# The first expert block on the seven-product scheme, with three sum banks and one side bank

## The chip, the cores and the metric

One core of one Trainium2 chip runs the whole program. The metric is the device time of one execution in microseconds. The engines are TensorE (PE, with its weight loads shown apart as PEld), VectorE (DVE), ScalarE (ACT), GpSimd (POOL) and SyncE (SP, which here issues nearly all the DMA transfers).

## The reference

Three stages follow one another: a feature-map attention, a dense layer pair, and a soft mixture of eight experts. Only the last one is touched by the change.

```python
def _moe2_ref(x, w_gate, w1, w2):            # x: 2304 x 512, w1: 8 x 512 x 1024, w2: 8 x 1024 x 512
    logits = x @ w_gate
    P = np.exp(logits - logits.max())
    for _ in range(8):                        # the balancing
        P /= P.sum(1, keepdims=True) + 1e-09
        P /= P.sum(0, keepdims=True) + 1e-09
        P *= N / E
    out = np.zeros((N, D))
    for e in range(E):
        ye = np.maximum(x @ w1[e], 0.0) @ w2[e]
        out += P[:, e:e + 1] * ye
    return out
```

## The kernel before

Every large product is made of three TensorE products (`mm3`, lines 79 to 82), since each operand is kept as a high and a low part. The expert stage runs over 16 blocks `b` (expert `e`, half `j` of its hidden columns), and each block over 3 units `c` of 768 tokens (`UP` = 3 pairs of token tiles). A unit (b, c) has a first product and a second one.

The first product (`hidden`) is a 2x2 block product in seven products (Strassen-Winograd). Its operands `t1, b11, b22, t2, b21, t3, t4` were stored to DRAM as `xs` by `operands` while the dense stage ended, and are read back through a ring of five buffers `xr`. Each of the seven is done for two column groups `q`, with 6 matmuls of 384 columns each, which makes 14 steps of one unit. Their sums live in banks `att` (2), `h` and `kv`.

The second product of a unit is interleaved with the 14 steps of the next unit. For blocks 1 to 15 it is again a seven-product scheme (`seconds`): seven operand pairs of `got` (made by `inner` and split into halves by ACT and POOL) and `w2t` (made by `w2_prep`), each for the three token pairs `i`, 6 matmuls of 256 columns each, so 126 matmuls a unit. DVE adds each result to `acc`. The sums lie in half banks of four PSUM banks `acc`. For block 0 (`b < FIRST`) it is the plain product (`outputs`): 6 token tiles a unit, 12 matmuls of 512 columns each, so 72 matmuls; ACT copies each result to `acc`. `w2_prep` then makes 4 weight tiles for block 0 and 7, with four extra sums (`combine`), for the other blocks.

In block 0 the gate logits are summed beside the first product (`gate_add`, 16 matmuls of 384 columns a unit) in a bank `acc` of its own and brought into token order by `gate_end`. The balancing, `sinkhorn`, is a generator with 11 stops. In the kernel before, both are advanced only inside `outputs` (lines 1039 to 1042), once for each call. The six calls that run in unit (1, 0) advance it four times, and nothing advances it later.

The scheduler of the framework orders the instructions of each engine's queue: by the place in the program text, lowered or raised by `high_priority`, and by when it expects operands and buffers to be free. Buffers with one tag share a number of slots: 8 for `w2o` (`W2B`), 14 for `h` (`HB`), 4 for `raw2`. The last two chunks of `operands` borrow slots of these: chunk 3 keeps its seven tiles `xo` in `w2o`, chunk 4 in `h`, until they are stored to `xs`.

Of the kernel before, what the change touches and what calls it, by code (L numbers as in the profile page):

```python
# [21 lines left out]
def tile_kernel(ctx: ExitStack, tc, q, k, v, w_phi, w_in, w_out, w_gate, w1, w2, out):  # L22
    nc = tc.nc
# [682 lines left out]
    FIRST = 1  # L706
# [57 lines left out]
    def w2_prep(b):  # L764
        def keep(o, src):
            w2t[b, o] = halves("w2o", W2B, src)

        if b < FIRST:
            for i in range(2 * QB):
                keep(i, raw.pop((b, True) + divmod(i, QB)))  # L770
                yield
            return
        (b11, b12), (b21, b22) = (tuple(raw.pop((b, True, r, k)) for k in range(2)) for r in range(2))
        keep("b11", b11)
        yield
# [12 lines left out]
        keep("b21", b21)  # L788
        yield
# [54 lines left out]
    out_pool = []  # L844
    lg = hp_.tile([P, NTT, E], F32, name="lg")
# [3 lines left out]
    def sinkhorn():  # L849
# [8 lines left out]
        ps = bank("acc")  # L858
# [3 lines left out]
        ps = bank("acc")  # L862
# [3 lines left out]
        for _ in range(NITER):  # L866
            nc.vector.tensor_reduce(out=r1, in_=pm, axis=AX.X, op=ALU.add)
            nc.vector.tensor_scalar(r1, r1, 1e-9, None, op0=ALU.add)
            nc.vector.reciprocal(out=r1, in_=r1)
            nc.vector.tensor_tensor(out=pm, in0=pm, in1=r1.unsqueeze(2).to_broadcast([P, NTT, E]), op=ALU.mult)  # L870
            nc.vector.tensor_reduce(out=c1, in_=pm.rearrange("p t e -> p e t"), axis=AX.X, op=ALU.add)
            yield
            ps = bank("acc")
# [24 lines left out]
    gate_ps = []  # L898
    GATE = {"t1": (0, 0), "b11": (0, 2 * E), "b22": (1, 0), "b21": (1, 4 * E)}

    def gate_add(x, kh, w0):
        first = not gate_ps
        if first:
            gate_ps.append(bank("acc"))
        for k in range(2):
            for h in range(2):
                nc.tensor.matmul(
                    gate_ps[0][0:4 * E, 0:UW], lhsT=wg[:, 2 * kh + k, w0:w0 + 4 * E], rhs=x[:, h, k, :],
                    start=first and k == 0 and h == 0, stop=True, skip_group_check=True,
                )  # L910

    def gate_end(c):
        lt = hp_.tile([4 * E, UW], F32, tag="u", name="lt", bufs=UB)
        nc.scalar.copy(lt, gate_ps.pop()[0:4 * E, 0:UW])
        yield
        ps = bank("acc")
        for i in range(UP):
# [4 lines left out]
            lg[:, 2 * UP * c:2 * UP * (c + 1), :], ps[:, 0:2 * UP * E].rearrange("p (t e) -> p t e", e=E)  # L922
# [3 lines left out]
    UB, HB = 10, 14  # L926

    side_work = []
# [54 lines left out]
    def hidden(b, c, n0, got):  # L983
# [11 lines left out]
        for i, o in enumerate(XOPS):  # L995
            x_ahead(n0 + i + XR)
            x = xring[n0 + i]
            for q in range(QB):
# [6 lines left out]
                if b == 0 and q == 0 and o in GATE:  # L1005
                    gate_add(x, *GATE[o])
# [6 lines left out]
                elif b >= FIRST:  # L1013
                    inner(b, o, q, T, got, ps, plus)
                elif o == "t2":
                    got["12", q] = relu_halves(plus("p53", q, ps))
                elif o == "b21":
                    T["c11", q] = plus("p1", q, ps)
                elif o == "t3":
                    got["22", q] = relu_halves(plus("p5", q, ps))  # L1020
                    if q == QB - 1:
                        for p in range(QB):
                            got["11", p] = relu_halves(T.pop(("c11", p)))
                else:
                    got["21", q] = relu_halves(ps)
                yield


    def outputs(b, ti, hs, t):
        _, acc, pm = out_pool  # L1030
        e, j = blocks[b]
        ps = bank("acc")
        ts_ = slice(t * P, (t + 1) * P)
        for i, h in enumerate(hs):
            w = w2t[b, i]
            mm3(ps, h[:, 0, ts_], h[:, 1, ts_], w[:, 0], w[:, 1], i == 0, i == 2 * QB - 1)
        a = acc[:, ti, :]
        nc.scalar.copy(a, ps)
        with tc.high_priority(offset=-100 if len(lg_done) == NUN else 50):
            if side_work and next(side_work[0], 1):  # L1040
                side_work.pop(0)
                lg_done.append(1)
# [5 lines left out]
    banks = []  # L1048

    def seconds(b, c, got):  # L1050
        _, acc, pm = out_pool
        e, j = blocks[b]
        if not banks:
            banks.extend(bank("acc") for _ in range(4))
# [3 lines left out]
        order = [SECOND[i] for i in ((0, 2, 1, 6, 4, 3, 5) if last else range(7))]  # L1058
        at_ = {
# [4 lines left out]
        if last:  # L1064
# [4 lines left out]
            }  # L1069
        seen, scaled = set(), set()  # L1070
        for ho, wo, ch, t, n in order:
            w = w2t[b, wo]
            due = []
            for i in range(UP):
                pb, half, first = at_[ch][i]
                first = bool(first) and ch not in seen
# [8 lines left out]
                for i_, ps in due:  # L1085
# [7 lines left out]
                    if e == 0:  # L1093
# [12 lines left out]
            seen.add(ch)  # L1106

    behind = []
    lg_done = []
    pending = None  # L1110
    n0 = 0
    for b, c in units:
        got = {}
        for i, _ in enumerate(hidden(b, c, n0, got)):
# [6 lines left out]
            elif odd and behind:  # L1121
                outputs(*behind.pop(0))
            if odd and c == NUN - 1 and b + 1 < len(blocks):
                take(coming, 1)
            if odd and c == 0 and b:
                take(late, 1)
        if not out_pool:
# [4 lines left out]
            take(w2_prep(0), 9)  # L1132
        n0 += len(XOPS)
        if b == 0:
            side_work.append(gate_end(c))
            next(side_work[-1])
            if c == NUN - 1:
                side_work.append(sinkhorn())
        if b >= FIRST:
            pending = seconds(b, c, got)  # L1140
        else:
            behind = [
                (b, 2 * (UP * c + i) + t, [got["%d%d" % (r, t + 1), q] for r in (1, 2) for q in range(QB)], i)
                for t in (1, 0) for i in range(UP)
            ]

        if c == 0:
            if b > 0:
                take(late, 9)
# [40 lines left out]
```

## Time and profile before

| | |
|---|---|
| median of 3 runs | 2093.19 us (2092.52 to 2093.55) |
| the profiled execution | 2092.61 us |
| its span, first to last instruction | 2090.8 us |
| PE busy | 2070.7 us, 99% |
| DVE, ACT, POOL busy | 67%, 44%, 57% |
| granted TensorE clock | 1.00 in every slice |

The span is the time between the first and the last instruction; the remaining 1.8 us of the execution lie around it. A share is an average over all stages. In the windows and timelines, times are counted from the span's start. The expert stage begins at 642 us.

### The profile page before, as it was taken

How to read it: one execution, taken by the hardware profiler on the slowest of the kernel's cores; microseconds unless marked ns; L12 is line 12 of the kernel's file. 1: busy time of each engine (PE TensorE's matmuls, PEld its weight loads, DVE VectorE, ACT ScalarE, POOL GpSimd, SP SyncE). 2: the span in 40 equal slices, each digit the busy share in tenths (PEclk: the TensorE clock that was granted, in tenths of full speed). 3: DMA queues.
4: the chain of work that ended last, by engine and by line, in shares of the span. 5: the costliest groups of instructions: out<-in, count | busy, mean ns of one | idle time of the engine just before them, and what ended most of it. 6: DMA issues, size and time to landing. Idle time of an engine off the chain costs nothing.

```text
span 2090.8 us, 36461 instructions
## 1 busy us (share of the span) xinstructions
PE 2070.7 (99%) x13433; PEld 1957.4 (94%) x13433; DVE 1395.0 (67%) x2547; ACT 922.6 (44%) x1892; POOL 1201.7 (57%) x1173
## 2 busy tenths in 40 slices
PE   8999999999999999999999999999999999999998
PEld 7787888888888899999999999999999999999998
DVE  8998765754324257766776677666776677667766
ACT  7776655654223334333433334333433343334432
POOL 2112211110301559987878788788787877879762
PEclk9999999999999999999999999999999999999999
DMA  8798565646736756565566655556556465654654
GB/s 264 256 331 284 173 189 167 203 140 217 262 121 194 249 177 226 212 213 211 181 222 226 213 202 205 208 211 232 197 212 222 172 233 220 216 214 175 241 189 135
DMA packets 194865, 440.02 MB, mean 210 GB/s; under 512 B 41448, under 2 KB 123496, under 8 KB 194688
## 3 DMA queue, kind: packets, MB, share of 16 engines
q1 hardware_dynamic: 190688, 428.19, 59.1%
q0 software_dynamic: 2560, 8.39, 1.0%
q8 instruction: 107, 1.75, 0.3%
q10 hardware_dynamic: 1440, 1.12, 0.2%
q14 instruction: 70, 0.57, 0.1%
HBM read 399.51 MB, written 38.12 MB: 209 GB/s over the span
## 4 chain that ended last, share of the span: by engine, by line
PE 92%; DVE 3%; ACT 2%; POOL 1%; issue 1%; DMA 1%; SPq 0%; POOLq 0%; DVEq 0%; ACTq 0%
PE ps_acc L82 14%; PE ps_acc L81 14%; PE ps_acc L80 13%; PE ps_att L80 6%; PE ps_att L81 6%; PE ps_att L82 6%; PE ps_h L80 6%; PE ps_h L82 6%; PE ps_h L81 6%; PE ps_kv L81 4%; PE ps_kv L80 4%; PE ps_kv L82 4%; PE ps_kv L86 1%; PE ps_att L86 1%; PE ps_acc L86 1%
## 5 line engine op out<-in xcount | busy, mean ns | idle before, releaser
L76 POOL TENSOR_TENSOR h<-u,h 128x384 fp32r<-128x384 f32 x450 | 509.1, 1149 | 169.8 <-ACT h L67 155.5
L81 PE MATMUL ps_acc<-w2o,h 128*128 128x256 f32 (+1 forms) x1950 | 557.0, 286 | 0.9 <-POOL w2o L76 0.8
L82 PE MATMUL ps_acc<-w2o,h 128*128 128x256 f32 (+1 forms) x1950 | 557.4, 286 | 0.4 <-POOL h L76 0.4
L80 PE MATMUL ps_acc<-w2o,h 128*128 128x256 f32 (+1 forms) x1950 | 555.2, 285 | 2.2 <-DVE acc L1097 1.7
L1097 DVE SCALAR_TENSOR_TENSOR acc<-ps_acc,pm,acc 128x256 f32<-128x256 f32 x876 | 378.7, 474 | 232.9 <-PE ps_acc L82 225.4
L67 ACT ACTIVATE h<-u 128x384 fp32r<-128x384 f32 x450 | 236.7, 526 | 328.6 <-DVE u L978 121.8
L81 PEld LDWEIGHTS ps_acc<-w2o,h 128*128 128x128 f32 x1950 | 368.4, 189 | 4.5 <-POOL w2o L76 2.2
L80 PEld LDWEIGHTS ps_acc<-w2o,h 128*128 128x128 f32 x1950 | 367.4, 188 | 5.2 <-DVE acc L1097 1.9
L82 PEld LDWEIGHTS ps_acc<-w2o,h 128*128 128x128 f32 x1950 | 369.0, 189 | 3.3 <-POOL h L76 0.6
L80 PE MATMUL ps_att<-xr,w1o 128*128 128x384 f32 x576 | 193.7, 336 | 0.0
L81 PE MATMUL ps_att<-xr,w1o 128*128 128x384 f32 x576 | 193.3, 336 | 0.0
L82 PE MATMUL ps_att<-xr,w1o 128*128 128x384 f32 x576 | 193.1, 335 | 0.0
L988 ACT COPY u<-ps_att 128x384 f32<-128x384 f32 x192 | 90.9, 474 | 153.5 <-PE ps_att L82 153.5
L736 POOL TENSOR_TENSOR ws<-raw,raw 128x512 f32<-128x512 f32 x62 | 84.7, 1366 | 118.4 <-DMA raw<-in_moe_w_dram 118.4
L80 PE MATMUL ps_h<-xr,w1o 128*128 128x384 f32 x384 | 129.4, 337 | 0.4 <-DVE u L978 0.4
L80 PE MATMUL ps_kv<-xr,w1o 128*128 128x384 f32 x384 | 128.9, 336 | 0.3 <-DVE u L992 0.3
L81 PE MATMUL ps_h<-xr,w1o 128*128 128x384 f32 x384 | 128.9, 336 | 0.0
L81 PE MATMUL ps_kv<-xr,w1o 128*128 128x384 f32 x384 | 128.8, 335 | 0.0
L82 PE MATMUL ps_h<-xr,w1o 128*128 128x384 f32 x384 | 128.8, 335 | 0.0
L82 PE MATMUL ps_kv<-xr,w1o 128*128 128x384 f32 x384 | 128.6, 335 | 0.0
L957 ACT ACTIVATE u<-u 128x384 f32<-128x384 f32 x90 | 47.3, 526 | 169.5 <-DVE u L992 169.5
L70 POOL TENSOR_SCALAR E<-E 128x1024 fp32r<-128x1024 f32 (+1 forms) x24 | 22.9, 954 | 155.6 <-ACT E L322 72.0
(285 smaller groups left out, 4842.1 us busy)
## 6 DMA issues: line engine op xcount, KB each, us to landing
xr<-xs_t SPq DMA_DIRECT2D x192, 768.0 KB, 4.8
xr<-xs_b SPq DMA_DIRECT2D x144, 768.0 KB, 4.9
w<-scratch SPq DMA_DIRECT2D x128, 512.0 KB, 4.2
raw<-in_moe_w_dram SPq DMA_DIRECT2D x128, 256.0 KB, 2.7
xs_t<-xo SPq DMA_DIRECT2D x36, 256.0 KB, 5.2
raw<-in_moe_w_in_dram SPq DMA_DIRECT2D x16, 512.0 KB
raw<-in_moe_w_out_dram SPq DMA_DIRECT2D x16, 512.0 KB, 4.1
scratch<-cw SPq DMA_DIRECT2D x32, 256.0 KB, 4.3
```

Of the source, the lines that this page charges most:

```text
L67: nc.scalar.activation(dst, src, AF.Copy, scale=scale)
L70: nc.gpsimd.tensor_scalar(dst, src, 1.0, 1.0, op0=ALU.mult, op1=ALU.mult)
L76: nc.gpsimd.tensor_tensor(out=dst, in0=src, in1=f32(hi), op=ALU.subtract)
L80: nc.tensor.matmul(o, lhsT=wh, rhs=xh, start=start, stop=False, skip_group_check=chk)
L81: nc.tensor.matmul(o, lhsT=wh, rhs=xl, start=False, stop=False, skip_group_check=chk)
L82: nc.tensor.matmul(o, lhsT=wl, rhs=xh, start=False, stop=stop, skip_group_check=chk)
L86: nc.tensor.matmul(o, lhsT=w[0], rhs=x[0], start=start, stop=stop, skip_group_check=chk)
L736: nc.gpsimd.tensor_tensor(out=t, in0=x, in1=y, op=op)
L957: nc.scalar.activation(t, t, AF.Relu)
L988: nc.scalar.copy(t, ps)
L1097: nc.vector.scalar_tensor_tensor(out=a, in0=ps, scalar=pm[:, ti, e:e + 1], in1=a, op0=ALU.mult, op1=ALU.add)
```

## The change

`FIRST` and `outputs` go. Block 0 runs through `inner`, `w2_prep` with seven tiles, and `seconds`, like the other blocks.

The four banks `acc` are taken once, before the first unit. The fourth, `side`, holds the gate's sums, the reordered logits and every product of the balancing; so in block 0 `seconds` has three banks for its sums. There it goes over the token pairs in two turns, first `i` = 0 and 1 for all seven products, then `i` = 2, with the product of `a12` and `b21` moved from the last to the fourth place. The first result for each half of a token tile is copied to `acc` by ACT, later ones are added by DVE.

The gate's first product is emitted one step later, `gate_end` inside the same unit (after `t3`, and after the first half of `t4`), and the balancing is advanced at each of the 14 steps of unit (1, 0) with a lowered priority, so that it runs through all its rounds. `w2_prep(0)` is advanced twice at each odd step from step 9 of unit (0, 0) on, and finished after the unit.

```diff
-    FIRST = 1
@@ w_load
-                if second and b >= FIRST:
+                if second:
...
-                elif second:
-                    f0 += k * P
-                    nc.sync.dma_start(t, w2[e, f0:f0 + P, :])
@@ w2_prep
-        if b < FIRST:
-            for i in range(2 * QB):
-                keep(i, raw.pop((b, True) + divmod(i, QB)))
-                yield
-            return
@@ before the expert stage
+    banks = [bank("acc") for _ in range(4)]
+    side = banks[3]
@@ sinkhorn (three places), gate_add, gate_end
-            ps = bank("acc")
+            ps = side
@@ hidden
-                if b == 0 and q == 0 and o in GATE:
-                    gate_add(x, *GATE[o])
+                if b == 0:
+                    if q == 0 and o in GATE and i:
+                        if o == "b11":
+                            gate_add(xring[n0], "t1")
+                        gate_add(x, o)
+                    elif (o, q) == GS:            # ("t3", 0)
+                        gate = gate_end(c)
+                        next(gate)
+                    elif (o, q) == GE:            # ("t4", 0)
+                        next(gate)
...
-                elif b >= FIRST:
+                else:
                     inner(b, o, q, T, got, ps, plus)
...
-    def outputs(b, ti, hs, t):
...
@@ seconds
+        turns = [range(UP)]
...
+        if b == 0:
+            order = [SECOND[i] for i in (0, 1, 2, 6, 3, 4, 5)]
+            turns = [range(UP - 1), range(UP - 1, UP)]
+            at_ = {
+                "a": [(b0, 0, 1), (b0, 1, 0), (b2, 0, 1)],
+                "x": [(b1, 0, 1), (b1, 1, 0), (b1, 0, 1)],
+                "y": [(b2, 0, 1), (b2, 1, 0), (b0, 0, 1)],
+            }
-        for ho, wo, ch, t, n in order:
+        for turn, (ho, wo, ch, t, n) in ((x, y) for x in turns for y in order):
...
-                    if e == 0:
+                    if b == 0 and (ti, n) not in begun:
+                        begun.add((ti, n))
+                        nc.scalar.copy(a, ps)
+                    elif e == 0:
                         nc.vector.tensor_tensor(out=a, in0=ps, in1=a, op=ALU.add)
@@ the loop over units
+    RB, L0 = -100, 9
+    late = w2_prep(0)
+    pending, balance = None, sinkhorn()
...
-            elif odd and behind:
-                outputs(*behind.pop(0))
+            if (b, c) == (1, 0):
+                with tc.high_priority(offset=RB):
+                    take(balance, 1)
...
-            if odd and c == 0 and b:
-                take(late, 1)
+            if odd and c == 0 and (b or i >= L0):
+                take(late, 1 if b else 2)
...
-            take(w2_prep(0), 9)
...
+        pending = seconds(b, c, got)
         if c == 0:
-            if b > 0:
-                take(late, 9)
+            take(late, 9)
```

## Rows read from the trace of the kernel before

**Rows 1.** Windows: start:end, length, busy PE PEld DVE ACT POOL, clock, DMA, GB/s
```profile
662.80:697.00 34.20, 32.84 (x160) 27.27 (x159) 7.58 (x13) 9.52 (x19) 13.19 (x12) 1.00 0.97 312
697.00:732.00 35.00, 35.00 (x180) 30.58 (x179) 10.06 (x15) 10.71 (x22) 22.18 (x22) 1.00 0.57 203
732.00:768.00 36.00, 35.69 (x182) 31.66 (x180) 16.48 (x27) 14.20 (x29) 14.92 (x13) 1.00 0.62 215
768.00:797.00 29.00, 28.89 (x206) 28.89 (x207) 22.39 (x48) 12.00 (x25) 23.99 (x23) 1.00 0.49 177
797.00:827.00 30.00, 30.00 (x216) 30.00 (x215) 19.83 (x38) 11.61 (x24) 27.11 (x27) 1.00 0.51 187
...
860.00:2050.00 1190.00, 1189.67 (x8444) 1189.46 (x8443) 831.51 (x1566) 466.15 (x965) 950.37 (x878) 1.00 0.58 211
```

**Rows 2.** Groups by line and shape, PE: the second product's two forms
```profile
L80 PE MATMUL ps_acc<-w2o,h 128*128 128x256 f32 x1878 | 527.5, 281 | 1.7 <-DVE acc L1097 1.7
...
L80 PE MATMUL ps_acc<-w2o,h 128*128 128x512 f32 x72 | 27.8, 395 | 0.5 <-POOL w2o L70 0.5
```

**Rows 3.** Timeline of PE: start, duration, line and form
```profile
682.24 0.40 PE L80 MATMUL ps_acc<-w2o,h 128*128 128x512 f32 x1
...
685.00 0.33 PE L80 MATMUL ps_att<-xr,w1o 128*128 128x384 f32 x1
...
769.29 0.28 PE L874 MATMUL ps_acc<-c,ones 128*128 128x8 f32 x2
...
769.63 0.28 PE L81 MATMUL ps_acc<-w2o,h 128*128 128x256 f32 x1
...
777.66 0.28 PE L80 MATMUL ps_acc<-w2o,h 128*128 128x256 f32 x1
...
779.08 0.34 PE L80 MATMUL ps_h<-xr,w1o 128*128 128x384 f32 x1
```

**Rows 4.** Timeline of POOL: start, duration, form, and the idle time before with its releaser
```profile
640.98 0.63 POOL L70 TENSOR_SCALAR w2o<-raw 128x512 fp32r<-128x512 f32 x1 [6.85 <-PE ps_acc L82]
641.69 1.30 POOL L76 TENSOR_TENSOR w2o<-raw,w2o 128x512 fp32r<-128x512 f32 x1
672.87 0.62 POOL L70 TENSOR_SCALAR w2o<-raw 128x512 fp32r<-128x512 f32 x1 [29.88 <-DMA xs_b<-xo]
...
756.05 10.21 POOL L76 TENSOR_TENSOR h<-u,h 128x384 fp32r<-128x384 f32 x8 [20.91 <-ACT h L67]
```

**Rows 5.** Timeline of SP's queue: DMA issues
```profile
674.88 0.39 SPq L724 DMA_DIRECT2D raw<-in_moe_w_dram  x1
...
681.55 4.46 SPq L578 DMA_DIRECT2D xs_t<-xo  x4
```

**Rows 6.** Waits of PE's weight loads, 640 to 860 us: total, times, longest
```profile
PEld ps_acc L81 <- POOL w2o L76: 2.2, 3, 0.8
...
PEld ps_h L80 <- DVE u L978: 0.8, 1, 0.8
```

**Rows 7.** One tile: the balancing's instructions that touch `pm`, with counts
```profile
L867 DVE TENSOR_REDUCE r<-pm x2: 303/303/303, 765.9 to 774.1; 128x18 f32<-128x144 f32 x2
...
L878 DVE TENSOR_TENSOR pm<-pm,c x1: 1072/1072/1072, 773.0 to 773.0; 128x144 f32<-128x144 f32 x1
```

**Rows 8.** Windows of one round, tile `r` (DVE), then tile `c` (PE, PEld, DVE)
```profile
765.80:774.05 8.25, 1.58 (x4) 1.00 0.36 128
...
765.80:774.05 8.25, 0.28 (x2) 0.36 (x2) 2.62 (x5) 1.00 0.36 128
```

**Rows 9.** Timeline of DVE around the start of POOL's splits
```profile
755.82 0.55 DVE L963 TENSOR_TENSOR u<-u 128x384 f32<-128x384 f32 x1
...
760.17 1.37 DVE L968 SCALAR_TENSOR_TENSOR u<-u 128x384 f32<-128x384 f32 x1
```

**Rows 10.** Groups by shape: copies and adds of half a bank, ACT and DVE
```profile
L563 ACT COPY xf<-ps_att 128x256 f32<-128x256 f32 x2 | 0.7, 373 | 1.2 <-POOL w2o L70 0.9 <-PE ps_att L82 0.3
...
L1094 DVE TENSOR_TENSOR acc<-ps_acc,acc 128x256 f32<-128x256 f32 x63 | 24.0, 417 | 14.9 <-PE ps_acc L82 14.6
```

More of the change, by code (lines that the diff above doesn't have):

```diff
@@ L861, in sinkhorn @@
         yield
-        ps = bank("acc")
+        ps = side
         nc.tensor.matmul(ps[:, 0:1], lhsT=ones[0:1, :], rhs=g2, start=True, stop=True)
@@ L872, in sinkhorn @@
             yield
-            ps = bank("acc")
+            ps = side
             nc.tensor.matmul(ps[:, 0:E], lhsT=ones, rhs=c1, start=True, stop=True)
@@ L895, in store, with gate_add @@
             c += n
-    gate_ps = []
     GATE = {"t1": (0, 0), "b11": (0, 2 * E), "b22": (1, 0), "b21": (1, 4 * E)}
[L901 to L904, printed above, removed]
+    def gate_add(x, o):
+        kh, w0 = GATE[o]
         for k in range(2):
@@ L907, in gate_add @@
                 nc.tensor.matmul(
-                    gate_ps[0][0:4 * E, 0:UW], lhsT=wg[:, 2 * kh + k, w0:w0 + 4 * E], rhs=x[:, h, k, :],
-                    start=first and k == 0 and h == 0, stop=True, skip_group_check=True,
+                    side[0:4 * E, 0:UW], lhsT=wg[:, 2 * kh + k, w0:w0 + 4 * E], rhs=x[:, h, k, :],
+                    start=o == "t1" and k == 0 and h == 0, stop=True, skip_group_check=True,
                 )
@@ L913, in gate_end @@
         lt = hp_.tile([4 * E, UW], F32, tag="u", name="lt", bufs=UB)
-        nc.scalar.copy(lt, gate_ps.pop()[0:4 * E, 0:UW])
+        nc.scalar.copy(lt, side[0:4 * E, 0:UW])
         yield
-        ps = bank("acc")
+        ps = side[:, UW:UW + 2 * UP * E]
         for i in range(UP):
@@ L921, in gate_end @@
         nc.vector.tensor_copy(
-            lg[:, 2 * UP * c:2 * UP * (c + 1), :], ps[:, 0:2 * UP * E].rearrange("p (t e) -> p t e", e=E)
+            lg[:, 2 * UP * c:2 * UP * (c + 1), :], ps.rearrange("p (t e) -> p t e", e=E)
         )
@@ L926, in tile_kernel @@
     UB, HB = 10, 14
-    side_work = []
+    GS, GE = ("t3", 0), ("t4", 0)
     def product(ps, w, x, q, fresh):
@@ L1012, in hidden @@
                     kept("p53", q, ps)
-                elif b >= FIRST:
+                else:
                     inner(b, o, q, T, got, ps, plus)
[L1015 to L1025, printed above, removed]
-                yield
-    def outputs(b, ti, hs, t):
[L1030 to L1042, printed above, removed]
+                yield
     SECOND = (
@@ L1047, in tile_kernel @@
     )
-    banks = []
     def seconds(b, c, got):
@@ L1052, in seconds @@
         e, j = blocks[b]
-        if not banks:
-            banks.extend(bank("acc") for _ in range(4))
         b0, b1, b2, b3 = banks
@@ L1069, in seconds @@
             }
+        if b == 0:
[6 more added lines that the diff above has]
+            }
         seen, scaled = set(), set()
-        for ho, wo, ch, t, n in order:
+        for turn, (ho, wo, ch, t, n) in ((x, y) for x in turns for y in order):
             w = w2t[b, wo]
             due = []
-            for i in range(UP):
+            for i in turn:
                 pb, half, first = at_[ch][i]
-                first = bool(first) and ch not in seen
+                first = bool(first) and (ch, turn) not in seen
                 ps = pb[:, half * HK:(half + 1) * HK]
@@ L1105, in seconds @@
                 yield
[L1106 to L1110, printed above, removed]
+            seen.add((ch, turn))
+    begun = set()
+    RB, L0 = -100, 9
+    late = w2_prep(0)
+    pending, balance = None, sinkhorn()
     n0 = 0
@@ L1131, in tile_kernel @@
             out_pool += [mo, mo.tile([P, NTT, DM], F32, name="acc"), mo.tile([P, NTT, E], F32, name="pm")]
-            take(w2_prep(0), 9)
         n0 += len(XOPS)
[L1134 to L1145, printed above, removed]
+        pending = seconds(b, c, got)
         if c == 0:
-            if b > 0:
-                take(late, 9)
+            take(late, 9)
             if b + 1 < len(blocks):
```

## The prediction

> **What bounds the kernel now.** I read the windows by stage first. From 860 to 2050 us PE is busy 1189.67 of 1190.00 us; DVE, POOL and ACT have 30, 20 and 61% of the time free [rows 1]. So in the expert stage PE's own stream sets the end, and other engines count only where PE waits for them. The change touches the three units of block 0 (their second products run from 662 to 769 us) and what follows directly. There PE is idle for 34.20 − 32.84 = 1.36 us in unit (0, 1), nothing in (0, 2), 0.31 us in (1, 0) and 0.11 us in (1, 1) [rows 1], 1.8 us together. The view of waits names the two causes: weight tiles `w2o` that POOL had not finished (2.2 us for the weight loads, part of it hidden), and one wait for DVE (0.8 us) while the balancing ran [rows 6]. A gain can therefore only come from a shorter PE stream plus at most those 1.8 us, and a loss from new waits of these two kinds.
>
> **The PE stream of block 0's second product.** Before, line 80 issues 72 matmuls of 512 columns [rows 2], and lines 81 and 82 as many: 72 a unit. Twelve of them in a row take 685.00 − 682.24 = 2.76 us, 0.230 us each [rows 3], so 16.56 us a unit. After, it is 126 matmuls of 256 columns. Twelve of these take 779.08 − 777.66 = 1.42 us, 0.118 us each [rows 3], so 14.91 us a unit. The scheme saves 1.65 us a unit, not an eighth of all, because two narrow matmuls take 0.237 us and one wide one 0.230 us. Over three units: **−4.95 us**. The gate's matmuls and the six that reorder the logits are the same in number and only move by a step or two; they cost nothing new. The later first gate product holds one `xr` slot for about a step (1 us) longer, which the five slots cover: a slot is used again only four operands, eight steps, later.
>
> **The balancing on PE.** Before, line 867 ran twice and line 878 once: one round and a half [rows 7]. After, all eight rounds run, so line 874 comes seven times more. Its pair of small matmuls and the slower start behind it take 769.63 − 769.29 = 0.34 us where the next matmul alone would have needed 0.12 us [rows 3]: 0.22 us each, **+1.5 us** for seven.
>
> **The balancing on DVE.** In the one whole round, the instructions on `r` take 1.58 us and those on `c` 2.62 us, 4.2 us together, and the round lasts 8.25 us from end to end [rows 8]. Six and a half more rounds are about 27 us of DVE. DVE has 19.5 us free in the window of (1, 0), 6.6 us in (1, 1) and 10.2 us in (1, 2) [rows 1]; the change takes 9 adds of 0.417 us [rows 10] = 3.8 us of the first. So the rounds need the free time of (1, 0) and (1, 1) to the last and part of (1, 2). They may have it: nothing reads `pm` before the scaling of block 0 and 1, whose program place is unit (2, 1), and the only other user of the side bank is the last product of unit (1, 0)'s second product, at the end of (1, 1). But PE's queue is in order: each of the eight matmuls of line 874 that stands earlier than DVE delivers stops the first and second products behind it, and DVE's late sums hold the banks `h` and `kv`, as in the 0.8 us wait [rows 6]. What makes DVE late is to be seen at 755 us: an instruction of 128x384 with both inputs in SBUF takes 0.55 us just before POOL's splits begin and 1.37 us beside them [rows 9, 4]. The Trainium skill (SBUF — State Buffer, "SBUF: two separate sides") says that DVE with two SBUF inputs and GpSimd take one shared port pair as an exclusive lock for a whole instruction; the trace agrees, 0.55 against 1.37 us, and by that rule the sum would only get worse, the more of the rounds fall beside the splits. Lower bound 0 (the early half of unit (1, 0) has little DVE work and no splits, since `gate_end` is now done before it). Upper bound seven waits of 0.8 us, 5.6 us. I take **+1.0 us**, nearer to the lower end, since (1, 0) has the most free time.
>
> **Weight tiles and slots in units (0, 0) and (0, 1).** A tile costs POOL 0.63 + 0.07 + 1.30 = 2.0 us [rows 4]. Before, there are four; the first is made at 641 us in the one `w2o` slot that no `xo` holds, and the second only at 672.87 us, when the stores of `xo` gave the next slots back [rows 4]. After, seven are needed, and four sums of about 1.3 us (the same shape and operation). By the program's order the tiles 2 to 4 take the slots of the first three `xo`, as before, and tiles 5 to 7 those of the next three. The stores of these are issued after 674.88 us, the last at 681.55 to 686.0 us [rows 5], while the DMA engines are busy 97% of the window [rows 1]. So `t1, t2, t3` come at 675, 677 and 679 us and `b22, t4, b21` between about 681 and 690 us. In before, SP also stops for the loads of the next w1, which wait for POOL to free `raw2` [rows 5]; these come later now, which may let the stores go earlier. POOL also has ten splits of unit (0, 0) at 1.28 us (10.21 / 8 [rows 4]); it is free before 672 us, so they are hidden. What PE has to do without `b21`: by 673 us about 3 steps of unit (0, 1) are left (3 us), then two steps and gate products of (0, 2) (3 us) and six of the seven products of turn one with the tiles as they come (6 x 1.4 = 8.5 us): enough to about 687 us, against 684 to 690 us. But `a12` x `b21` stands fourth in the new order and its tile is made last, and turn two needs its bank, so the `h` slots of unit (0, 0) return only behind it. Lower bound: the 1.36 us of before vanishes (−1.4). Upper bound: PE has used up its work at 684 us and waits to 692 us, +8. I take **+1.0 us**.
>
> **What I cost at nothing.** ACT loses 18 wide copies and gets 36 half copies of 0.373 us [rows 10], 13 us over three units in which it has 24 us free in each [rows 1]. DVE's 27 adds lie in units where it is idle over half the time. The sums in three banks: between two uses of one bank there is at least one product of another chain and one step of the first product, 0.7 + 1.0 us, against an add of 0.417 us. Block 1's tiles: before, four of them were made in (0, 2); now turn two holds the slots until the end of (1, 0), which moves some 6 to 8 us of POOL work to a window where POOL has 2.9 to 21 us free [rows 1]. They are needed one by one over 29 us, so the cover is there; gone, it would cost up to 3 us.
>
> **Sum.** 2092.61 − 4.95 + 1.5 + 1.0 + 1.0 = 2091.2 us for the profiled execution. The median of the runs is 0.6 us above it, so I forecast **2091.8 us**, −0.07%. A measurement of this kernel can tell about 0.2% (4.2 us) from no change.
>
> **Rivals.** *Everything hides* (faster): the 1.8 us of idle time go and neither new wait appears: −4.95 + 1.5 − 1.8 = −5.2, 2088.0 us. For it: DVE's early half of (1, 0) is free and the tiles are asked for piecemeal. Against it: three more slots are needed than the stores gave back by 673 us. *The balancing holds PE* (slower): DVE becomes the bound from 732 to 797 us; with 1.2 us for each of seven rounds, 8 us instead of 1: 2099 us. It decides when the rounds added take more than the 22 us that DVE has free there; at 4.2 us a round they do, and (1, 2) must take the rest. *Late tiles* (slower): PE runs dry between about 684 and 692 us, 8 us instead of 1: 2099 us. It decides if `b21` comes later than 688 us; the store row that ends at 686.0 us speaks for it, the greedy order of PE's queue against it.
>
> **Chances.** Forecast (2088.8 to 2097.4 us) 0.53; everything hides 0.20; the balancing holds PE 0.14; late tiles 0.13. That gives faster 0.20, same 0.53, slower 0.27. The range runs from just below the best case to one slow rival with some of the other, 2087.3 to 2101 us; the forecast's own is 2089 to 2096 us.
>
> **What would show it.** Matmuls of 512 columns gone from the expert stage and 378 of 256 columns more; line 874 in eight pairs; the waits on `w2o` by POOL below 3 us and around 675 to 692 us; DVE over 90% busy from 735 to 790 us with no wait of PE over 1 us at line 874 or at the banks `h` and `kv`. Wrong would be a PE idle time of more than 4 us in 660 to 700 us or in 732 to 830 us, or a steady stage that no longer runs at 1189.67 of 1190 us.

## The result and the profile after

The changed kernel takes 2118.59 us (median of 4 runs, 2118.34 to 2119.48); the kernel before took 2092.86 us beside it (2092.34 to 2093.55). The ratio is 1.012 (95% interval 1.0109 to 1.0132): 1.2% slower, 25.7 us, and outside my range, which ended at 2101.0. The profiled execution took 2118.34 us with a span of 2116.2 us; the mean granted clock fell from 1.000 to 0.995. Profiled executions do not all reach the expert stage at the same time: a copy of DVE that stands at 642.1 us in the kernel before comes 0.7 us later here and up to 4.0 us later in the runs below, in most of the late ones behind a granted clock of 0.57 to 0.68 from 204 to 208 us.

The windows of the changed kernel, with the columns of [rows 1]; the first is the end of unit (0, 0), the last the steady stage:

```profile
642.10:662.80 20.70, 18.19 (x104) 15.97 (x102) 19.33 (x34) 13.30 (x30) 7.52 (x7) 1.00 0.82 267
662.80:697.00 34.20, 32.10 (x190) 29.15 (x189) 14.26 (x24) 13.72 (x33) 25.16 (x25) 0.90 0.75 221
697.00:732.00 35.00, 31.70 (x215) 30.03 (x215) 16.43 (x28) 12.58 (x30) 26.46 (x25) 1.00 0.68 250
732.00:768.00 36.00, 34.68 (x233) 33.89 (x232) 18.39 (x41) 17.39 (x43) 18.30 (x17) 0.95 0.54 182
768.00:797.00 29.00, 23.54 (x140) 22.30 (x138) 27.61 (x61) 9.40 (x22) 26.96 (x26) 0.88 0.32 111
797.00:827.00 30.00, 27.87 (x187) 27.55 (x187) 25.76 (x62) 10.63 (x22) 21.88 (x22) 0.94 0.54 192
917.00:2080.00 1163.00, 1162.22 (x8247) 1161.77 (x8247) 813.72 (x1528) 453.38 (x940) 922.94 (x849) 1.00 0.58 210
```

The steady stage is untouched (PE 1162.22 of 1163.00 us). Nearly everything is lost between 642 and 830 us, and in two forms. PE is idle: 2.5, 2.1, 3.3, 1.3, 5.5 and 2.1 us in the six windows, 16.8 us, where [rows 1] had 1.8 from 662.8 on. And the granted clock, 1.00 in every slice before, is 0.88 to 0.95 in four of them. Finer windows show how the two belong together:

```profile
656.00:660.00 4.00, 3.15 (x17) 2.37 (x15) 3.77 (x8) 2.83 (x6) 0.00 (x0) 1.00 0.98 358
660.00:664.00 4.00, 2.35 (x12) 2.12 (x12) 4.00 (x7) 2.71 (x6) 3.61 (x4) 0.85 1.09 315
664.00:668.00 4.00, 4.00 (x14) 3.96 (x15) 3.58 (x6) 1.80 (x5) 2.95 (x3) 0.50 1.02 312
...
772.00:776.00 4.00, 1.55 (x8) 1.55 (x9) 3.97 (x7) 1.65 (x4) 4.00 (x4) 0.93 0.37 155
776.00:780.00 4.00, 4.00 (x20) 3.91 (x19) 4.00 (x7) 1.27 (x4) 4.00 (x5) 0.64 0.00 0
780.00:784.00 4.00, 1.69 (x11) 1.26 (x10) 3.93 (x9) 0.72 (x2) 4.00 (x4) 1.00 0.01 2
784.00:788.00 4.00, 4.00 (x21) 4.00 (x22) 3.92 (x10) 1.75 (x5) 3.92 (x5) 0.71 0.65 238
```

A stretch in which PE works little is followed by one in which it is busy throughout and does half as much: 14 matmuls from 664 to 668 us at a granted clock of 0.50, which is 1.2 GHz. PE's busy time hides this loss; only the clock and the counts show it. PE's timeline, with the waits (idle before, and releaser) at the ends of its lines:

```profile
661.65 0.41 PE L80 MATMUL ps_h<-xr,w1o 128*128 128x384 f32 x1 [2.35 <-POOL h L76]
...
665.09 0.52 PE L82 MATMUL ps_kv<-xr,w1o 128*128 128x384 f32 x1
665.40 0.52 PE L80 MATMUL ps_kv<-xr,w1o 128*128 128x384 f32 x1
...
774.45 0.39 PE L867 MATMUL ps_acc<-c,ones 128*128 128x8 f32 x2 [3.01 <-DVE c L864]
...
783.93 0.39 PE L867 MATMUL ps_acc<-c,ones 128*128 128x8 f32 x2 [2.10 <-DVE c L864]
```

From 664.8 us on, matmuls of 384 columns start every 0.32 us, where they start every 0.17 us at full clock. The four largest of PE's waits from 630 to 900 us (total, times, longest) are:

```profile
PE ps_acc L867 <- DVE c L864: 7.1, 3, 3.0
PE ps_acc L80 <- DVE acc L1075: 2.8, 2, 2.6
PE ps_h L80 <- POOL h L76: 2.4, 1, 2.4
PE ps_acc L81 <- POOL w2o L76: 1.7, 3, 0.8
```

The balancing's product (line 867, before 874) waits for DVE. The second product waits for DVE's adds out of its half banks. The first product of unit (0, 0) waits behind POOL's splits. Of these only the last was there before: 0.8 us in the same view, and for the weight loads 2.2 us [rows 6] against 2.5 now. The next two, not shown, are 1.3 us for an ACT copy out of a half bank and 0.7 us for a load of `xr`.

What PE has to do did change as the diff says. In the groups by form the 512-column matmuls of [rows 2] are gone, and line 80 has 2004 of 256 columns, 126 more:

```profile
L80 PE MATMUL ps_acc<-w2o,h 128*128 128x256 f32 x2004 | 565.8, 282 | 6.2 <-DVE acc L1075 2.8 <-DVE acc L1078 1.7 <-ACT acc L1073 1.3
```

A lag by unit: the instruction of DVE that closes a unit's first product (`h<-ps_kv`) comes in units (0, 0), (0, 1), (0, 2), (1, 0) and (1, 1) 11.6, 12.7, 12.8, 16.7 and 24.4 us later than before, and stays near that. This counts DVE's lateness, and 0.7 us of it came before the stage. What PE itself loses is its idle time and, for the clock, its busy time by one minus the granted clock. Summed over windows of 4 us, for this kernel, the kernel before and five of the runs below (us):

| | 640 to 672 | 672 to 712 | 712 to 768 | 768 to 830 |
|---|---|---|---|---|
| before | 0.0 | 1.4 | 0.3 | 0.1 |
| after | 5.7 | 5.4 | 3.0 | 12.4 |
| e3 | 3.8 | 8.4 | 2.8 | 11.3 |
| e15 | 4.2 | 7.1 | 3.5 | 2.3 |
| e16 | 2.1 | 2.3 | 2.8 | 0.8 |
| e17 | 2.2 | 1.4 | 2.8 | 0.8 |
| e18 | 0.0 | 1.7 | 2.7 | 0.9 |

In the changed kernel the first stretch ends about where unit (0, 0) does, the second about where (0, 1) does, and the balancing runs mostly in the last. So some 11 us are lost over units (0, 0) and (0, 1), half of them in each, and 12 us while the balancing runs.

### The profile page after: what moved, and what is told of

It reads as the page before. It is cut to its first block, busy times and chain, and to the rows that moved or that the text cites. A ratio compares the mean times of both kernels' runs of the same rounds, so it can differ in the third digit from the quotient of the medians.

```text
span 2116.2 us, 37035 instructions
## 1 busy us (share of the span) xinstructions
PE 2080.0 (98%) x13609; PEld 1973.0 (93%) x13609; DVE 1440.0 (68%) x2644; ACT 935.7 (44%) x1940; POOL 1246.6 (59%) x1213
## 4 chain that ended last, share of the span: by engine, by line
PE 87%; DVE 5%; ACT 2%; POOL 2%; DMA 2%; issue 1%; SPq 0%; ACTq 0%; POOLq 0%; DVEq 0%
PE ps_acc L82 13%; PE ps_acc L81 13%; PE ps_acc L80 13%; PE ps_att L80 6%; PE ps_att L81 6%; PE ps_att L82 6%; PE ps_h L80 5%; PE ps_h L81 5%; PE ps_h L82 5%; PE ps_kv L81 4%; PE ps_kv L80 4%; PE ps_kv L82 4%; PE ps_kv L86 1%; PE ps_att L86 1%; POOL h L76 1%
## 5 line engine op out<-in xcount | busy, mean ns | idle before, releaser
L76 POOL TENSOR_TENSOR h<-u,h 128x384 fp32r<-128x384 f32 x480 | 542.8, 1149 | 157.5 <-ACT h L67 136.3
L80 PE MATMUL ps_acc<-w2o,h 128*128 128x256 f32 x2004 | 565.8, 282 | 6.2 <-DVE acc L1075 2.8
L81 PE MATMUL ps_acc<-w2o,h 128*128 128x256 f32 x2004 | 565.8, 282 | 1.7 <-POOL w2o L76 1.7
L82 PE MATMUL ps_acc<-w2o,h 128*128 128x256 f32 x2004 | 566.3, 283 | 0.4 <-POOL h L76 0.4
L67 ACT ACTIVATE h<-u 128x384 fp32r<-128x384 f32 x480 | 252.1, 526 | 349.2 <-DVE u L968 123.3
L80 PEld LDWEIGHTS ps_acc<-w2o,h 128*128 128x128 f32 x2004 | 380.0, 190 | 8.1 <-DVE acc L1075 3.2
L81 PEld LDWEIGHTS ps_acc<-w2o,h 128*128 128x128 f32 x2004 | 380.8, 190 | 2.5 <-POOL w2o L76 2.5
L82 PEld LDWEIGHTS ps_acc<-w2o,h 128*128 128x128 f32 x2004 | 381.2, 190 | 0.6 <-POOL h L76 0.6
```

The lines of the kernel that those rows point to most:

```text
L67: nc.scalar.activation(dst, src, AF.Copy, scale=scale)
L76: nc.gpsimd.tensor_tensor(out=dst, in0=src, in1=f32(hi), op=ALU.subtract)
L80: nc.tensor.matmul(o, lhsT=wh, rhs=xh, start=start, stop=False, skip_group_check=chk)
L81: nc.tensor.matmul(o, lhsT=wh, rhs=xl, start=False, stop=False, skip_group_check=chk)
L82: nc.tensor.matmul(o, lhsT=wl, rhs=xh, start=False, stop=stop, skip_group_check=chk)
```

## The experiments

My first theory was that two of the three rivals' causes hold at once, the balancing and something in unit (0, 0); the rival to it was that one cause, late weight tiles or the three banks, makes all of it. Medians of the kernel before lay between 2093.2 and 2094.0 us in these comparisons.

**The balancing.** e1 is the changed kernel with one and a half rounds, as many as the kernel before ran:

```diff
-            if (b, c) == (1, 0):
+            if (b, c) == (1, 0) and i < 4:
```

> The changed kernel with the balancing advanced only in the first four steps of unit (1, 0), so that it runs one round and a half as in the kernel before; the other six and a half rounds are left out. Theory B (the added rounds hold PE through DVE and line 867, and the stalls lower the granted clock): the lag that units (1, 0) and (1, 1) add, 3.8 + 7.8 us, goes, so about 2107 us, and the granted clock stays 1.00 from 764 us on. Theory S (the loss comes from the start, units (0, 0) to (0, 2), and is only handed on): no more than the 1.5 us of PE work of line 867, about 2117 us.

2112.55 us, ratio 1.009 (1.0073 to 1.0107): 6 us better, and 19 us still lost. That lies between the two theories; the clock does stay at 1.00 from 764 us on, as theory B said. e2 puts the rounds alone into the kernel before:

```diff
+            if (b, c) == (1, 0) and i >= 2:
+                with tc.high_priority(offset=-100):
+                    take(balance, 1)
...
-                side_work.append(sinkhorn())
+                balance = sinkhorn()
```

> The kernel before, with the balancing alone taken over from the change: it is advanced at each step of unit (1, 0) and runs all eight rounds. Theory B: the rounds cost about the same here, 8 to 12 us, so 2101 to 2105 us, with waits of PE at line 874 for DVE and a clock below 1.00 behind them. Theory S: they cost 2 us or less without the changed block 0, about 2095 us.

2110.91 us, 1.0082 (1.0067 to 1.0097). By themselves the rounds cost 17 us, more than either theory said, with 9.1 us of waits at line 874. Three windows of it:

```profile
768.00:772.00 4.00, 1.41 (x4) 1.26 (x5) 2.93 (x13) 0.21 (x1) 0.00 (x0) 0.73 0.01 5
772.00:776.00 4.00, 4.00 (x11) 3.09 (x10) 1.65 (x6) 0.00 (x0) 0.00 (x0) 0.50 0.00 0
776.00:780.00 4.00, 1.23 (x7) 1.06 (x6) 2.41 (x10) 0.58 (x1) 0.00 (x0) 0.91 0.00 0
```

POOL does nothing there and DVE is not full: PE and DVE hand a round to each other, and the rest of PE's queue stands behind it. e5 is e2 without the round's product on PE (the column sums stay unsummed over the partitions):

```diff
-            nc.tensor.matmul(ps[:, 0:E], lhsT=ones, rhs=c1, start=True, stop=True)
-            nc.vector.tensor_scalar(c1, ps[:, 0:E], 1e-9, None, op0=ALU.add)
+            nc.vector.tensor_scalar(c1, c1, 1e-9, None, op0=ALU.add)
```

> The kernel before with all eight rounds of the balancing, as in the run e2, but without the matmul of line 874: the column totals stay within each partition. DVE does the same number of operations. Theory Q (the rounds cost because line 874 stands in PE's queue in order and waits for a DVE that is late): most of the 17 us goes, 2094 to 2099 us, and the clock stays at 1.00. Theory D (DVE is occupied so long that its sums hold the banks of the first product): it stays over 2105 us.

2104.6 us, 1.0049 (1.0032 to 1.0066). That is between the range of theory Q and that of theory D, so neither holds alone. Without the product on PE 6 of the 17 us go. The other 11 stay with the rounds on DVE alone: PE now waits 5.6 us for DVE's adds to `acc` and 2.6 us for its sums `u`. (The instruction that adds 1e-9 reads SBUF here instead of PSUM and takes up to 0.74 us, against 0.17 at most in e2, so a part of the 11 may be new.)

If density were the trouble, spreading would help. e10 does it on the changed kernel, e12 on the kernel before (there from step 5 of (1, 0) to step 5 of (2, 0)):

```diff
-            if (b, c) == (1, 0):
+            if i % 4 == 1 and i < 13 + 14 * ((b, c) == (1, 0)) and (1, 0) <= (b, c) <= (2, 0):
```

> The changed kernel with one edit: the balancing is advanced at every fourth step of units (1, 0) to (2, 0) instead of at each step of (1, 0); all eight rounds stay. Theory D (the rounds cost because they come too densely for DVE: 4.2 us of DVE work in 1 us of program): the waits at line 867 and most of what the rounds cost on the changed kernel (6 us by e1) go, 2110 to 2114 us. Rival W (the DVE work itself costs, wherever it falls, since every unit needs DVE): 2116 to 2120 us, with new waits of PE for DVE in (1, 1) to (2, 0).

> The kernel before with all eight rounds of the balancing, advanced at every fourth step from step 5 of unit (1, 0) to step 5 of (2, 0), against each step from 2 on in e2 (2110.9 us). Theory D (too dense for DVE): 2094 to 2099 us. Rival W (the 27 us of DVE work cost wherever they fall): 2106 to 2112 us.

e10: 2133.24 us, 1.0182 (1.0165 to 1.0199), 15 us worse than dense. e12: 2115.66 us, 1.0101 (1.0086 to 1.0116), 5 us worse than e2. Both are slower than either theory said. Spreading moves the rounds to where POOL splits. One instruction shows what that does, line 877, which scales 8 elements a partition; the duration is given as least/median/most, first in e2, then in e12:

```profile
L877 DVE TENSOR_SCALAR c<-c x8: 164/172/1080, 760.8 to 791.5; 128x8 f32<-128x8 f32 x8
```

```profile
L877 DVE TENSOR_SCALAR c<-c x8: 160/998/1261, 783.2 to 866.5; 128x8 f32<-128x8 f32 x8
```

Each of these sixteen that takes over 0.18 us overlaps an instruction of POOL with two inputs; those with none beside them take 0.16 to 0.17 us. And the timeline of e12 shows the price, 5.86 us of PE behind one round:

```profile
827.40 1.26 DVE L877 TENSOR_SCALAR c<-c 128x8 f32<-128x8 f32 x1
...
832.51 0.96 DVE L868 TENSOR_SCALAR r<-r 128x18 f32<-128x18 f32 x1
...
837.06 0.59 PE L874 MATMUL ps_acc<-c,ones 128*128 128x8 f32 x2 [5.86 <-DVE c L871]
```

A second difference is not separated: spread rounds also use a bank (`banks[3]`) that the second product's sums of `a12` and `b21` then need. The waits at the round's product, 7.7 us in e12, are put down to `c` and not to the bank.

e13 (on e11, below) and e14 (on e2) leave out the small instruction that adds 1e-9 to the row sums and fold line 877 into the reading of PSUM:

```diff
-            nc.vector.tensor_scalar(r1, r1, 1e-9, None, op0=ALU.add)
...
-            nc.vector.tensor_scalar(c1, ps[:, 0:E], 1e-9, None, op0=ALU.add)
+            nc.vector.tensor_scalar(c1, ps[:, 0:E], float(E) / NT, 1e-9 * E / NT, op0=ALU.mult, op1=ALU.add)
...
-            nc.vector.tensor_scalar(c1, c1, float(NT) / E, None, op0=ALU.mult)
```

> The changed kernel with block 0 in one turn (e11, 2114.4 us) and two of the nine DVE instructions of a round taken out: the one that adds 1e-9 to the row sums is left out, and the scaling by 2304/8 is folded into the one that reads the column sums from PSUM. Both are tiny (18 and 8 elements a partition) and have all operands in SBUF. Theory P (the rounds cost because DVE's instructions with all operands in SBUF wait beside POOL's: in the changed kernel these two take 0.395 and 0.554 us on average, 7.6 us for eight rounds, against 0.17 us at best): 2110 to 2112 us, and the waits at line 867 fall from 5.8 to about 3 us. Rival N (the number of products that PE's queue must wait for decides; these stay eight): 2114 to 2115 us.

> The kernel before with all eight rounds from step 2 of unit (1, 0) on (e2, 2110.9 us), each without the same two DVE instructions as in e13. In e2 most of the rounds ran before POOL's splits (median 0.176 and 0.172 us for these two, longest 0.98 and 1.08). Theory P: some 3 us for the rounds beside splits, and as much for the idle and lowered-clock time behind them, 2104 to 2108 us. Rival N: 2110 to 2111 us.

e14: 2106.72 us, 1.0064 (1.0049 to 1.0079), 4 us better than e2 and inside what theory P, that of the slowed instructions, gave; the two intervals overlap a little, the single times do not. e13: 2112.76 us (2111.38 to 2116.18), 1.0095 (1.008 to 1.011); its wait at the round's product fell from 5.8 to 4.1 us, but the time falls between the two theories, and against e11 it can't be told apart.

**The weight tiles and the order.** e3 keeps POOL's sums for the tiles behind the splits of unit (0, 0); e4 drops the new order of the seven products:

```diff
-        t2 = combine(b22, t1, ALU.subtract)                # e3; t3 likewise
+        t2 = combine(b22, t1, ALU.subtract, b == 0)        # b == 0: held in program order
...
-    RB, L0 = -100, 9
+    RB, L0 = -100, 99
```

```diff
-            order = [SECOND[i] for i in (0, 1, 2, 6, 3, 4, 5)]
```

> The changed kernel with the weight sums t2 and t3 of block 0 held behind POOL's splits of unit (0, 0), so that POOL does not work beside DVE from 647 to 652 us. Theory S1 (these sums stretch DVE's operand work of the last chunks by 2.5 us, which becomes PE's 2.35 us stall at 661 us and the half clock behind it): 4 to 6 us less, about 2113 us, and 1.00 of the clock from 660 to 672 us. Theory S2 (DVE has too much work there anyway, four more sums of the inner step): the stall stays over 1.5 us and the time within 1.5 us of 2118.6.

> The changed kernel with the seven products of block 0 in the order of the other blocks, so that the product of a12 with b21, the tile that is made last, stands last again. If the early place of b21 holds the h slots and so the first products (2.6 us wait at 707 us, 1.6 us at 676 to 684 us): 2 to 5 us less, 2114 to 2117 us. If these waits come from POOL's total of tiles and splits: within 1.5 us of 2118.6, or slower, since two products of chain a then follow each other on one bank.

e3: 2119.49 us, 1.0125 (1.011 to 1.014), as its theory S2 said. DVE's instructions are no longer stretched there, and PE loses 3.8 us by 672 us instead of 5.7; but a wait of 2.2 us for DVE's `u` is left, and from 672 to 712 us it loses 8.4 us instead of 5.4, since POOL now makes the tiles then. e4: 2122.04 us, 1.0136 (1.0121 to 1.0151), slightly worse. Neither moving the sums nor the old order gains anything in the total.

**The scheme without gate and balancing.** e6, e7 and e8 leave the gate's products, their reordering and the balancing out (`pm` is the constant 0.125). e6 does nothing else, e7 also gives block 0 four banks and one turn, and e8 besides makes the seven tiles by 14 plain copies on POOL, without their sums and low parts:

```diff
-                if b == 0:                    # gate (e6)
+                if False:
...
-        if b == 0:                            # banks, turns, order (e7)
+        if False:
...
+        if b == 0:                            # tiles (e8)
+            for o, src in (("b11", b11), ("t1", b12), ("t2", b22), ("t3", b12), ("b22", b22), ("t4", b21), ("b21", b21)):
+                t = w2t[b, o] = hp_.tile([P, 2] + list(src.shape[1:]), F32R, tag="w2o", name="w2o", bufs=W2B)
+                hi_pool(t[:, 0], src)
+                hi_pool(t[:, 1], src)
```

> The changed kernel without the gate's products, the reordering of the logits and the balancing (pm is set to a constant); three sum banks as in the change. PE has 48 gate matmuls of 0.174 us, 18 small ones and the rounds less, some 12 us. If only the scheme in three banks and the tiles were at fault, the 19 us of the run e1 stay: 2112.6 - 11 = about 2101 us. If the side work is needed for the stalls: below 2090 us.

> As the run e6, without the gate and the balancing, but block 0's sums in four banks, in one turn and in the order of the other blocks. Theory N (three banks and two turns make PE wait for adds, and hand the h slots back late): 8 us or more less than e6. Theory M (POOL's tiles and splits are late and slow DVE beside them, whatever the banks): within 3 us of e6.

> As the run e7, and block 0's seven weight tiles are made without the four sums and without the low parts: 14 copies of 0.62 us in POOL instead of 4 sums of 1.30, 7 of 0.62 and 7 of 1.30 us, 18.6 - 8.7 = 10 us less of POOL, and no operation with two inputs. Theory M: 4 us or more less than e7. If the slots of w2o (which wait for the stores of xo) are what is late: within 2 us of e7.

e9 is the point to measure them from, the kernel before without the same parts:

```diff
-                if b == 0 and q == 0 and o in GATE:
+                if False:
...
-        if b == 0:
-            side_work.append(gate_end(c))
-            next(side_work[-1])
-            if c == NUN - 1:
-                side_work.append(sinkhorn())
+        if b == 0 and c == 0:
+            nc.vector.memset(out_pool[2], 0.125)
```

> The kernel before without the gate and the balancing: no gate products, no reordered logits, pm filled with the constant 0.125, so its result leaves the weighting by the gate out. It is the reference point for e6, e7 and e8, which leave out the same. Theory S (the scheme in block 0 saves 5 us of PE columns, and its three banks and its weight tiles cost more than that): the 48 gate products of 384 columns at 0.16 to 0.17 us and some small ones go, 8 to 10 us, so about 2084 us, 10 us below e7 (2094.4) although e7's PE stream is 5 us shorter. Rival C (the four banks and the light tiles of e8 show the true price of the plain form): about 2091 us, 5 us above e8 (2086.5).

e9 took 2084.25 us (0.9952, 0.9937 to 0.9967), e8 2086.49 (0.9966, 0.9955 to 0.9978), e7 2094.37 (1.0004, 0.9994 to 1.0013), e6 2104.92 (1.0054, 1.0039 to 1.0069). The ranges of theory N (e7), theory M (e8) and theory S (e9) held; e6 is slower than its text expected. Read as steps: gate and balancing cost the kernel before 9 us. The scheme with light tiles is 2 us slower than the plain product, though its stream is shorter. Full tiles add 8 us, three banks in two turns 10.5 us, and gate with balancing 13.7 us, of which 9 were there before. The steps can't be carried over one by one: in e7 and e6 PE waits 10.9 and 10.3 us for `w2o`, so *Late tiles* happens there, where the changed kernel waits 2.1 us.

**The two turns.** e11 lets block 0 go over its token pairs in one turn, still in three banks:

```diff
-            order = [SECOND[i] for i in (0, 1, 2, 6, 3, 4, 5)]
-            turns = [range(UP - 1), range(UP - 1, UP)]
...
+            order = [SECOND[i] for i in (0, 1, 2, 3, 5, 4, 6)]
+            at_["y"] = [(b0, 0, 1), (b0, 1, 0), (b1, 0, 1)]
```

> The changed kernel with one edit: block 0's second product goes over its three token pairs in one turn, as the other blocks do, still in three banks (the chain of a12 x b21 reuses the half banks of the a chain after t4, and b22 stands between t4 and b21). Theory T (of the 10.5 us between e6 and e7 most is the two turns: the slots of h and the weight tiles are held to the end of the second turn, and one half bank is asked for again after only 0.7 us): 2108 to 2112 us. Rival B (three banks are the cost, whatever the order): 2117 to 2121 us.

2114.43 us, 1.0096 (1.008 to 1.0111), between the two theories: 4 us, against 10.5 from e6 to e7. e15 is e11 with e1's edit:

> The changed kernel with both edits that gained so far: block 0 in one turn (e11: -4.2 us) and one and a half rounds as before (e1: -6 us). If the two causes are separate: 2108 to 2109 us. If they are one (DVE late for the half banks, which both relieve): about 2112 us. What is left over the kernel before would then be the weight tiles and the first unit.

2108.54 us, 1.0071 (1.0055 to 1.0088): 10 us below the changed kernel, the sum of the two, so the gains are separate. Of what e15 still loses, 11.3 us fall in units (0, 0) and (0, 1), and 5.8 us behind them (the table above).

**The first two units.** All three start from e15. e16 takes the four plain operands in unit (0, 0) in place of the scheme's seven (four sums and their splits left out), e17 the light tiles of e8, and e18 both:

```diff
+                elif (b, c) != (0, 0):
                     inner(b, o, q, T, got, ps, plus)
+                elif o == "t2":
+                    got["a12", q] = got["s3", q] = relu_halves(plus("p53", q, ps))
...
```

> Base: e15 (one turn, one and a half rounds, 2108.5 us). Edit: in unit (0, 0) alone the seven operands of the second product are replaced by the four plain ones of the kernel before, each used where it fits (a12 for s3 too, a22 for s2, a21 for s1 and s4); the four sums and their splits by ACT and POOL are left out, and 8 slots of h are asked for in this unit instead of 14. PE's work is the same. Theory H (in unit (0, 0) the splits and the h slots that chunk 4's operands still hold stop PE, 13.4 us by the lag at the end of the first product): the wait of 2.4 us for POOL's h at 661 to 664 us goes with the lowered clock behind it, 2098 to 2103 us. Rival M (the weight tiles alone, which POOL makes and PE waits for, hold this unit): 2107 to 2109 us.

> Base: e15. Edit: block 0's seven weight tiles are made by 14 plain copies on POOL, without sums and low parts (as in e8). Theory H: little, 2105 to 2108 us, since POOL's tile work in unit (0, 0) stands ahead of the stall. Rival M: the 7.9 us between e7 and e8 return, 2100 to 2101 us.

> Base: e15, with the edits of e16 and e17 both. If the two causes are separate their gains add up, and what is left over the kernel before (2093.2 us) is the three banks' own price less the 5 us of columns saved: 2091 to 2095 us. If both take away the same wait, about the better of e16 and e17.

e16: 2097.65 us, 1.0012 (1.0003 to 1.0021). e17: 2096.51 us, 1.0011 (1.0002 to 1.002). e18: 2093.48 us, 0.9998 (0.9989 to 1.0008). Each edit alone gives 11 to 12 us, both 15, not 23: mostly a shared cause. e16 and e17 come out below every range given for them, and e18 lies in the range for two separate causes, although the gains do not add up. By the table 2 us of each gain fall before 672 us, 5 to 6 us from 672 to 712 us and 2 us behind that. The windows around the end of (0, 0), for the kernel before, then e15, e16 and e17:

```profile
656.00:664.00 8.00, 8.00 (x47) 7.11 (x46) 5.54 (x13) 3.68 (x9) 0.00 (x0) 1.00 0.97 306
664.00:672.00 8.00, 8.00 (x43) 7.10 (x44) 0.20 (x1) 1.92 (x4) 0.00 (x0) 1.00 1.04 303
```

```profile
656.00:664.00 8.00, 5.71 (x32) 4.67 (x30) 7.77 (x15) 5.31 (x11) 1.04 (x1) 1.00 0.99 346
664.00:672.00 8.00, 7.78 (x40) 7.52 (x41) 7.39 (x10) 4.70 (x11) 6.95 (x7) 0.79 1.03 315
```

```profile
656.00:664.00 8.00, 6.01 (x34) 5.31 (x34) 7.57 (x17) 4.72 (x11) 0.00 (x0) 1.00 0.96 313
664.00:672.00 8.00, 8.00 (x53) 7.46 (x52) 0.94 (x3) 3.29 (x8) 2.80 (x3) 1.00 1.06 302
```

```profile
656.00:664.00 8.00, 8.00 (x50) 7.72 (x50) 7.89 (x12) 4.44 (x10) 5.93 (x5) 1.00 1.05 329
664.00:672.00 8.00, 5.80 (x37) 5.06 (x36) 4.12 (x6) 5.75 (x15) 6.24 (x7) 1.00 1.06 320
```

DVE is nearly full from 656 to 664 us in these three, and was not in the kernel before. In e15 it stays so to 672 us beside 6.95 us of POOL; in e16 and e17 it is soon free, PE has one gap of about 2 us in these windows, and the clock stays at 1.00. What e16 still waits for is mostly the price of three banks, six waits of up to 1.4 us (e7, with four banks, has none of this kind):

```profile
PE ps_acc L80 <- DVE acc L1081: 5.6, 6, 1.4
```

## Why the prediction was wrong, step by step

**What bounds the kernel; the PE stream.** Held. PE's stream sets the end, and the loss came by new waits of PE, as the text said a loss would. Two of its three signs of being wrong came: PE was idle for 4.5 us from 660 to 700 us and for 8.9 us from 732 to 830 us; the steady stage held. The saving is there too, as the comparison of e9 with e8 and e7 shows, where no gate and no rounds are in the way. I took the sums of the table over the whole span. From e9 to e8 the span grew by 2086.1 − 2081.9 = 4.2 us, the idle time by 27.2 − 23.2 and the clock's loss by 5.5 − 0.0 us; without these it would be 5.3 us shorter. For e7, by the same sum (34.6 and 3.5 us, span 2092.7), it is 4.1 us. I had 4.95.

**"It is free before 672 us, so they are hidden."** This is the step that failed most. I asked when POOL would have the tiles ready for unit (0, 1), and called the ten splits of unit (0, 0) covered because POOL had been idle there. But DVE was not free: it makes the last operands `xo` of the dense stage just then, and the sum has no term at all for DVE's new sums of `inner`. DVE's timeline in the kernel before, with POOL idle:

```profile
648.22 0.42 DVE L73 TENSOR_TENSOR xo<-xt,xo 128x256 fp32r<-128x256 f32 x1
648.67 0.69 DVE L572 TENSOR_TENSOR xt<-xf,xt 128x512 f32<-128x512 f32 x1
```

The same two in the changed kernel, beside instructions of POOL of 1.3 to 1.6 us (two sums and a low part of a tile), and then one alone:

```profile
648.78 1.51 DVE L73 TENSOR_TENSOR xo<-xt,xo 128x256 fp32r<-128x256 f32 x1
...
651.35 1.67 DVE L572 TENSOR_TENSOR xt<-xf,xt 128x512 f32<-128x512 f32 x1
...
653.54 0.68 DVE L73 TENSOR_TENSOR xo<-xf,xo 128x512 fp32r<-128x512 f32 x1
```

POOL's new work (the tiles' sums first, the splits behind) and DVE's new sums of `inner` meet there, PE runs dry at 656 to 664 us behind the splits, and the clock falls: 5.7 us of PE by 672 us, and 5.4 more in (0, 1). e16 to e18 put the whole of weight tiles and slots in these units at 11 to 15 us; I had 1.0. Moving the tiles' sums (e3) only shifts the loss into (0, 1); making the tiles cheaper (e17) takes POOL's time away, 5.09 against 7.75 us from 672 to 680 us. Which part of POOL's work holds (0, 1) no run separates. The tiles themselves were as forecast: making `b21` starts at 688.57 us, and PE's waits for `w2o` are 2.1 us. *Late tiles* had nearly the right price, but the place was wrong.

**"The sums in three banks", costed at nothing.** The room I gave each half bank, 0.7 + 1.0 us, was set against the add's own 0.417 us. What counts is the time until DVE comes to the add, and DVE's queue holds instructions of over 1 us beside POOL's splits. Without the gate it cost 10.5 us together with the two turns (e6 to e7). On the changed kernel one turn instead of two gains 4 us (e11); what the three banks cost there beside it is not shown alone, but it would fit the 5 us by which e18 fails to show the saved columns.

**The balancing.** I had 1.5 us on PE and 1.0 on DVE. It costs 6 us on the changed kernel (e1, and e11 to e15) and 17 on the kernel before (e2). The forecast had DVE over 90% busy from 735 to 790 us; it was so only later, 27.61 of 29 us from 768 to 797 us (18.39 of 36 us in the window before), and not without waits at the round's product. The rival *The balancing holds PE* had the mechanism and the place. My lower bound rested on "the early half of unit (1, 0) has little DVE work and no splits"; e2 shows that a round there still stops PE, which has nothing to pass in front of it. That the same rounds cost less on the changed kernel may be because they then overlap waits that are there anyway; no run separates that. The Trainium skill (SBUF — State Buffer, "SBUF: two separate sides") says that GpSimd and certain forms of DVE instruction shut each other out of one port pair for a whole instruction. The trace agrees: line 877, from SBUF to SBUF, goes from 0.172 to 0.998 us in the median between e2 and e12, while the form that reads PSUM (line 875) takes at most 0.17 us in both.

**The clock.** My sum has no term for it. By the same sums the changed kernel is idle for 36.2 us against 20.0 before, and loses 9.6 us against 0.0 to the clock: 25.7 us, where its span is 25.4 us longer. Idle time of 16 us came with 10 more. Since the shorter stream less the added rounds should have given 3.4 us back, some 3 us of the loss show in neither sum, and no run says where they are.

**The account.** Forecast 2091.2 for the profiled execution, measured 2118.34, 27 us apart: weight tiles and slots in (0, 0) and (0, 1) 11 to 15 against 1.0; banks and turns about 10 against 0, of which 4 are shown on the changed kernel; balancing 6 against 2.5; the stream as forecast where the gate is left out. Each of these measured figures holds its share of the lowered clock. The prediction gives the forecast's own range in two forms, 2088.8 to 2097.4 and 2089 to 2096 us; the measured time lies above both. No version tried beats the kernel before by more than a measurement can tell, save e8 and e9, which leave the gate out.

## What to carry to other kernels

Idle time of an engine is only cover if the engines that share its data or ports are free too: before moving work to POOL, look at what DVE does in the same microseconds. Cost a reuse of a buffer by the delay until the freeing engine gets to it, not by the length of the freeing instruction. And where PE's stream sets the end, price a row of waits of 2 to 3 us above its length (here 10 us on 16, though after single waits of 2.0 and 2.2 us in e16 and e17 the clock stayed at 1.00), since the slower clock behind it does not show in the idle time.

## What I had not expected of the hardware

After PE's gap of 2.35 us at 659 to 662 us the granted clock was 0.50 from 664 to 668 us although PE was busy throughout. After a single gap of 2.24 us in e3, with full work before it, it was 0.50 from 670 to 672 us; after one of 2.20 us in e17, one of 1.99 us in e16 and one of 1.68 us in e9 it stayed at 1.00. So gaps of almost one length went either way, and what decides is not shown. An instruction of DVE on 8 elements a partition took between 0.160 and 1.261 us, and was long only beside an instruction of POOL.
